# The first twelve steps' leaky ReLU: a maximum on VectorE, or a sum on GpSimd

## The chip, the core and the metric

The kernel runs on one core of a Trainium2 chip. The core has five engines that run side by side, each with its own queue of instructions that it takes strictly in order: TensorE (PE in the profile, its weight loads PEld), VectorE (DVE), ScalarE (ACT), GpSimd (POOL) and SyncE (SP), which here only issues DMAs. The metric is the device time of one execution in microseconds (us), as the median of several runs.

## The reference

Attention over 8 batches, 8 heads, 576 tokens and head size 64 feeds a feed-forward layer with 4608 tokens, model width 512 and 2048 hidden units:

```python
out_up    = repeat(softmax_attention(mean4(q), mean4(k), mean4(v)), 4)   # on 144 averaged tokens
out_local = attention over the keys at distance < 4
x = (out_up + out_local) as [4608, 512]
h = x @ w_in                                        # [4608, 2048]
g = maximum(h, 0) + alpha * minimum(h, 0)           # leaky ReLU, one slope alpha per hidden unit
out = g @ w_out                                     # [4608, 512]
```

All of it is in 32-bit floats. The kernel keeps that precision by splitting each operand of a large product into a high and a low part (names ending in h and l) and adding three products.

## The kernel before, in words

The tokens of the feed-forward layer are cut into 18 chunks of 256 (`T`), the hidden units into 16 blocks of 128. A *step* `st` does two hidden blocks of one chunk; there are 144 steps, eight to a chunk. Each step goes through five functions:

- `hidden(st)` (L743): 24 matmuls on TensorE make h of 128 x 512 in a PSUM tile `ph` (two buffers).
- `slopes(st)` (L756): ScalarE reads h twice for each block. `t` gets slope times h (L760), and h itself is overwritten with sign times h (L761). The columns `sign` (+1 or -1) and `slope` (alpha times sign) are made at the start, in `load_alpha`; the sign of a hidden unit with alpha above 1 is also multiplied into `w_out`.
- `larger(st)` (L763): VectorE takes the maximum of the two, which is the leaky ReLU up to that sign.
- `split(st)` (L766): ScalarE copies the result to `gh`, GpSimd subtracts to get `gl` (the helper `sub`, L69).
- `product(st)` (L786): 12 matmuls on TensorE add the step's share to the output tiles `o`. After eight steps `finish` copies these out through the tiles `sg` (L804).

Around the steps runs the attention. The first batch is done ahead of step 0. While the first steps run, three other things are in progress. The weights' last blocks are taken apart into high and low parts by `make` (L161): ScalarE starts each block (`temp<-raw`, L184), VectorE does four passes (L188 to L194) and a subtraction (L207 or L211), and ScalarE makes the high part in between (`wih`, `woh`, L199 and L203). The averaged attention of the next batches goes through `down` (L224) in pieces: GpSimd folds loaded rows together (`ld`, `s2q`, `s2k`, `s2v`, the helper `add`, L72), TensorE transposes (`qkT`, L250), ScalarE copies (`qd`, `kd`), TensorE makes the scores (`s`, L263), VectorE the maximum (`dnb`, L267), ScalarE exponentials and a scaling (`dp`, L273 and L282), TensorE transposes (`pT`, L287), ScalarE copies (`th`, L291), TensorE multiplies (`pv`, L297). These pieces share two PSUM banks (`bank("d", ...)`), so that a transpose waits for the copy that empties the bank. And the local attention of unit 3 (`local`, L566) begins on VectorE near step 9.

The order on each engine is written by hand: each function is put in a list with a time in steps (`at(s - 1.45, slopes, s)`, `at(s - 1.15, larger, s)`, `at(s - 1.0, split, s)`, L861 to L866), the list is sorted by that time, and the instructions are issued in that order. Only the part ahead of it, with the first batch and the first five pairs of weight blocks, is ordered by a scheduler, which may also set its last instructions among those of step 0 and step 1.

The tile `xf` (L665) of 128 x 512 in the pool `late` has one buffer and is written for the first time in unit 3, near step 13. The pool `late` takes over the memory of the pool `start`, in which the first batch lived.

Of the kernel before, what the change touches and what calls it, by code (L numbers as in the profile page):

```python
# [9 lines left out]
F32 = mybir.dt.float32  # L10
F32R = mybir.dt.float32r
I32 = mybir.dt.int32
AF = mybir.ActivationFunctionType
ALU = mybir.AluOpType
# [11 lines left out]
NF = DF // 128  # L26
# [16 lines left out]
T0_DEC, D_DEC = 0.5, 0.56  # L43
UNITS = {3: 7.5, 4: 12.2, 5: 17.4, 6: 22.7, 7: 28.0}
U_STEP = 5.92
BY_HALF = (5, 9, 13, 17, 21)
FAR = {3: 2, 4: 2, 5: 2, 6: 2}

# [2 lines left out]
def tile_attention_moe(ctx: ExitStack, tc: tile.TileContext, q, k, v, w_in, w_out, alpha, out):  # L51
    nc = tc.nc

    const = ctx.enter_context(tc.tile_pool(name="const", bufs=1))
# [16 lines left out]
    def add(o, a, b):  # L71
        nc.gpsimd.tensor_tensor(o, a, b, op=ALU.add)  # L72
# [33 lines left out]

    sign = const.tile([128, NF], F32, name="sign")
    slope = const.tile([128, NF], F32, name="slope")

    def load_alpha():  # L110
        nc.sync.dma_start(slope, alpha.rearrange("(f p) -> p f", p=128))
        nc.vector.tensor_scalar(sign, slope, 1.0, 2.0, op0=ALU.is_le, op1=ALU.mult)
        nc.vector.tensor_scalar(sign, sign, -1.0, None, op0=ALU.add)
        nc.vector.tensor_tensor(slope, slope, sign, op=ALU.mult)


    wi, wo = ([[None] * 4, [None] * 4] for _ in range(2))
# [448 lines left out]
    def local(u, t0, t1):  # L566
        b, jj = u // 3, u % 3
        st = {}
        near = 7 - FAR.get(u, 1)
        by_half = u in BY_HALF  # L570
        groups = ((0, 3), (3, 3)) if by_half else ((0, 4), (4, 2))
# [169 lines left out]
    gs, outs, hs = {}, {}, {}  # L741
# [13 lines left out]

    def slopes(st):  # L756
        t = gs[st] = two.tile([128, 2, T], F32, tag="t", name=f"t{st}")
        for j in range(2):
            f = 2 * (st % NP) + j
            nc.scalar.activation(t[:, j], hs[st][:, j], AF.Copy, scale=slope[:, f:f + 1])  # L760
            nc.scalar.activation(hs[st][:, j], hs[st][:, j], AF.Copy, scale=sign[:, f:f + 1])  # L761

    def larger(st):  # L763
        nc.vector.tensor_tensor(gs[st], hs.pop(st), gs[st], op=ALU.max)  # L764

    def split(st):  # L766
        t = gs[st]
# [59 lines left out]


    load_alpha()
    rest = two.tile([128, DM], F32, tag="stage", name="rest", bufs=SB)[:, 0:4 * (S - 2 * T)]  # L830
    rest = rest.rearrange("p (a n) -> p a n", a=4)
    nc.gpsimd.memset(qd32, 0.0)
    with tc.tile_pool(name="start", bufs=1) as start:
# [20 lines left out]
        def at(t, f, *args):  # L854
            events.append((t, len(events), f, args))
# [3 lines left out]
    late = ctx.enter_context(tc.tile_pool(name="late", bufs=1))  # L859

    for s in range(NS):  # L861
        at(s - 1.95, hidden, s)
        at(s - 1.45, slopes, s)
        at(s - 1.15, larger, s)
        at(s - 1.0, split, s)
        at(s + 0.6, product, s)  # L866
        if s % NP == NP - 1:
            at(s + 1.02, finish if s + 1 < NS else finish_last, s // NP)
# [20 lines left out]
    for u in range(len(UNITS) + 3, 3 * B + 1):  # L889
        begin[u] = begin[u - 1] + U_STEP  # L890
    for b in range(2, B):
# [8 lines left out]
    for u in range(3, 3 * B + 1):  # L900
        if u < 3 * B:
            when, *mine = local(u, begin[u], begin[u + 1])
        else:
            when = {"before 0": begin[u] + 0.8, "before 1": begin[u] + 1.2}
        if put and u - 1 in BY_HALF:
            at(begin[u] + 0.3, flip, 1)
# [36 lines left out]
```

## Time and profile before

| what | value |
|---|---|
| median of 3 runs | 1014.16 us (1013.35 to 1014.5) |
| the profiled execution's own time | 1012.62 us |
| its span | 1010.8 us, 17864 instructions |
| PE busy | 960.6 us (95%) |
| DVE busy | 832.8 us (82%) |
| ACT busy | 560.2 us (55%) |
| POOL busy | 482.1 us (48%) |

A share over the whole span is an average over stages. Step 0's matmuls begin at about 85 us, the twelfth step's slopes (step 11) at 168 us. What the change touches lies between these two. From there to the end TensorE has few gaps.

### The profile page before, as it was taken

The numbers are of one execution on the slowest core, as the hardware profiler recorded it, in microseconds if no ns is written. First come the engines' busy times: TensorE is split into PE (matmuls) and PEld (weight loads), VectorE is DVE, ScalarE is ACT, GpSimd is POOL, SyncE is SP. The second block draws the span as 40 slices with busy tenths as digits, with TensorE's granted clock in tenths as the row PEclk, the third lists the DMA queues.
The fourth block names the chain that finished last, engine by engine and source line by source line (L and its number), as shares of the span: only waits on it lengthen the run. The fifth ranks groups of instructions, "written<-read, shape, count | busy, mean of one in ns | idle before, by whom it ended". The sixth has DMA issues, their size and how long they took to land.

```text
span 1010.8 us, 17864 instructions
## 1 busy us (share of the span) xinstructions
PE 960.6 (95%) x6402; PEld 852.7 (84%) x6402; DVE 832.8 (82%) x1347; ACT 560.2 (55%) x1483; POOL 482.1 (48%) x612
## 2 busy tenths in 40 slices
PE   5877989999999999999999999999999999999998
PEld 4756878898888898988888888888988898989997
DVE  6899988899888899899888898898898899997111
ACT  4767766465565555555455555555555554444442
POOL 2040645677665546555554544656555543323221
PEclk9856989999999999999999999999999999999999
DMA  8946443232422322433322332322331412210000
GB/s 191 222 148 242 123 153 98 83 119 83 145 83 73 118 81 78 121 97 93 103 88 66 100 111 71 125 80 74 123 100 60 131 49 61 86 43 22 1 21 22
DMA packets 61218, 98.26 MB, mean 97 GB/s; under 512 B 21578, under 2 KB 26954, under 8 KB 61130
## 3 DMA queue, kind: packets, MB, share of 16 engines
q1 hardware_dynamic: 60938, 96.87, 32.0%
q8 instruction: 50, 0.82, 0.3%
q10 hardware_dynamic: 192, 0.26, 0.1%
q14 instruction: 38, 0.31, 0.1%
HBM read 87.67 MB, written 9.44 MB: 96 GB/s over the span
## 4 chain that ended last, share of the span: by engine, by line
PE 72%; DVE 15%; ACT 4%; issue 3%; DMA 2%; POOL 2%; SPq 2%; DVEq 0%; ACTq 0%; POOLq 0%
PE o L798 33%; PE h L752 33%; DMA raw<-in_moe_w_out 2%; DVE qk L591 2%; DVE lb L650 2%; PE s L263 2%; DVE t L764 1%; PE pv L297 1%; DVE ls L595 1%; DVE temp L193 1%; DVE pv L647 1%; PE xp L659 1%; PE pT L287 1%; DVE temp L194 1%; DMA ld<-in_q 1%
## 5 line engine op out<-in xcount | busy, mean ns | idle before, releaser
L69 POOL TENSOR_TENSOR gl<-t,gh 128x512 fp32r<-128x512 f32 x144 | 186.5, 1295 | 390.8 <-ACT gh L769 347.4
L760 ACT ACTIVATE t<-h,slope 128x256 f32<-128x256 f32 x288 | 136.3, 473 | 203.0 <-PE h L752 166.2
L764 DVE TENSOR_TENSOR t<-h,t 128x512 f32<-128x512 f32 x144 | 99.0, 687 | 113.2 <-ACT h L761 108.6
L752 PE MATMUL h<-xh,wih 128*128 128x256 f32 x1152 | 190.9, 287 | 0.7 <-ACT xh L518 0.7
L798 PE MATMUL o<-woh,gh 128*128 128x512 f32 x576 | 188.1, 407 | 0.4 <-ACT woh L203 0.4
L752 PE MATMUL h<-xl,wih 128*128 128x256 f32 x1152 | 183.7, 281 | 0.6 <-POOL xl L69 0.6
L752 PE MATMUL h<-xh,wil 128*128 128x256 f32 x1152 | 184.1, 282 | 0.0
L798 PE MATMUL o<-wol,gh 128*128 128x512 f32 x576 | 182.1, 397 | 0.1
L798 PE MATMUL o<-woh,gl 128*128 128x512 f32 x576 | 182.1, 397 | 0.0
L752 PEld LDWEIGHTS h<-xh,wih 128*128 128x128 f32 x1152 | 163.5, 190 | 10.5 <-issue 1.8
L72 POOL TENSOR_TENSOR ld<-ld 72x256 f32<-72x256 f32 x168 | 125.4, 747 | 73.9 <-DMA ld<-in_q 49.4
L752 PEld LDWEIGHTS h<-xl,wih 128*128 128x128 f32 x1152 | 156.9, 190 | 0.8 <-POOL xl L69 0.8
L752 PEld LDWEIGHTS h<-xh,wil 128*128 128x128 f32 x1152 | 157.3, 190 | 0.0
L769 ACT CAST gh<-t 128x512 fp32r<-128x512 f32 x144 | 89.1, 619 | 118.7 <-DVE t L764 68.4
L595 DVE TENSOR_REDUCE ls<-qk 128x12 f32<-128x768 f32 (+1 forms) x126 | 136.4, 1083 | 2.8
L798 PEld LDWEIGHTS o<-woh,gl 128*128 128x128 f32 x576 | 108.6, 189 | 26.4
L798 PEld LDWEIGHTS o<-wol,gh 128*128 128x128 f32 x576 | 108.4, 188 | 26.4 <-DVE wol L211 0.7
L761 ACT ACTIVATE h<-h,sign 128x256 f32<-128x256 f32 x288 | 126.4, 439 | 0.0
L650 DVE TENSOR_TENSOR lb<-lb,pv 128x384 f32<-128x384 f32 x202 | 113.9, 564 | 5.5
L798 PEld LDWEIGHTS o<-woh,gh 128*128 128x128 f32 x576 | 98.3, 189 | 16.3 <-issue 2.2
L647 DVE TENSOR_TENSOR pv<-v,lb 128x1152 f32<-128x1152 f32 x84 | 93.6, 1115 | 2.6
L591 DVE TENSOR_TENSOR qk<-k,qp 128x768 f32<-128x768 f32 (+1 forms) x78 | 84.0, 1077 | 0.0
(148 smaller groups left out, 1111.4 us busy)
## 6 DMA issues: line engine op xcount, KB each, us to landing
k<-in_k SPq DMA_DIRECT2D x41, 384.0 KB
v<-in_v SPq DMA_DIRECT2D x41, 384.0 KB
raw<-in_moe_w_in SPq DMA_DIRECT2D x16, 512.0 KB
raw<-in_moe_w_out SPq DMA_DIRECT2D x16, 512.0 KB
ld<-in_q SPq DMA_DIRECT2D x56, 144.0 KB
ld<-in_k SPq DMA_DIRECT2D x56, 144.0 KB
ld<-in_v SPq DMA_DIRECT2D x56, 144.0 KB
q<-in_q SPq DMA_DIRECT2D x42, 192.0 KB
```

The costliest lines, as they stand in the source:

```text
L69: nc.gpsimd.tensor_tensor(o, a, b, op=ALU.subtract)
L72: nc.gpsimd.tensor_tensor(o, a, b, op=ALU.add)
L591: nc.vector.tensor_tensor(st["pr"][:, :nd], window(tiles[u, "k"], half, d0, nd), st["qp", half].unsqueeze(1).to_broadcast([128, nd, 2, 192 ...
L595: nc.vector.tensor_reduce(out=st["s"][:, half, d0:d0 + nd, :].rearrange("p a b -> p (a b)"), in_=st["pr"][:, :nd].rearrange("p a h (t d) - ...
L647: nc.vector.tensor_tensor(st["pr"][:, :nd], window4(tiles[u, "v"], half, d0, nd), prob(half, d0, nd), op=ALU.mult)
L650: nc.vector.tensor_tensor(st["acc"], st["acc"], st["pr"][:, i], op=ALU.add)
L752: nc.tensor.matmul(ph[:, j], w[:, m, 128 * o:128 * o + 128], x[:, m, :], start=(i == 0), stop=(i == 11))
L760: nc.scalar.activation(t[:, j], hs[st][:, j], AF.Copy, scale=slope[:, f:f + 1])
L761: nc.scalar.activation(hs[st][:, j], hs[st][:, j], AF.Copy, scale=sign[:, f:f + 1])
L764: nc.vector.tensor_tensor(gs[st], hs.pop(st), gs[st], op=ALU.max)
L769: nc.scalar.copy(gh, t)
L798: nc.tensor.matmul(outs[c][m], g[:, j, 128 * m:128 * m + 128], wo[w][n][:, o, :], start=(f == 0 and i == 0), stop=(f == NF - 1 and i == 2))
```

## The change

For the first twelve steps (`EARLY = 12`) the leaky ReLU is formed as a sum: with `gain` = sign - slope, which is never negative, max(sign h, slope h) is slope h + relu(gain h). ScalarE writes slope times h to `t` as before, and relu(gain h) to a tile `sh` in SBUF, which is the one buffer of the tag `xf`. GpSimd adds the two. The other 132 steps are unchanged.

```diff
+EARLY = 12
...
+        nc.vector.tensor_tensor(gain, sign, slope, op=ALU.subtract)
...
     def slopes(st):
         t = gs[st] = two.tile([128, 2, T], F32, tag="t", name=f"t{st}")
+        other = hs[st]
+        if st < EARLY:
+            other = late.tile([128, 512], F32, tag="xf", name=f"sh{st}").rearrange("p (j n) -> p j n", j=2)
         for j in range(2):
             f = 2 * (st % NP) + j
             nc.scalar.activation(t[:, j], hs[st][:, j], AF.Copy, scale=slope[:, f:f + 1])
-            nc.scalar.activation(hs[st][:, j], hs[st][:, j], AF.Copy, scale=sign[:, f:f + 1])
+            if st < EARLY:
+                nc.scalar.activation(other[:, j], hs[st][:, j], AF.Relu, scale=gain[:, f:f + 1])
+            else:
+                nc.scalar.activation(other[:, j], hs[st][:, j], AF.Copy, scale=sign[:, f:f + 1])
+        if st < EARLY:
+            hs[st] = other

     def larger(st):
-        nc.vector.tensor_tensor(gs[st], hs.pop(st), gs[st], op=ALU.max)
+        if st < EARLY:
+            add(gs[st], hs.pop(st), gs[st])
+        else:
+            nc.vector.tensor_tensor(gs[st], hs.pop(st), gs[st], op=ALU.max)
```

The order of the matmuls and of SyncE's DMAs is the same as before. On the other engines it moves at these places (numbers in names are buffers; a slope, `t`, `sh` and `gl` of the same step stand near each other).

ScalarE at steps 0 and 1, before: `t<-h,slope` and `h<-h,sign` of the two halves of step 0, then a weight block (`temp`), and so on to step 1 and to the exponentials (`dp,dsm`) of a piece of the averaged attention.

```order
L760 ACTIVATE t_995<-h_970,slope 128x256
L761 ACTIVATE h_970<-h_970,sign 128x256
L760 ACTIVATE t_995<-h_970,slope 128x256
L761 ACTIVATE h_970<-h_970,sign 128x256
L184 ACTIVATE temp<-raw_4_881 128x1024
...
L761 ACTIVATE h_1011<-h_1011,sign 128x256
L273 ACTIVATE dp_0_1060,dsm_0_1055<-s_0_1042,dnb_0_1054 96x144 x3
L275 ACTIVATE dsm_0_1055<-dsm_0_1055 96x3
L203 ACTIVATE woh_889<-temp,sign 128x512 x2
L769 CAST gh_1065<-t_1048 128x512
```

The same place now:

```order
L766 ACTIVATE t_997<-h_972,slope 128x256
L187 ACTIVATE temp<-raw_4_883 128x1024
L768 ACTIVATE sh_998<-h_972,gain 128x256
L766 ACTIVATE t_997<-h_972,slope 128x256
L768 ACTIVATE sh_998<-h_972,gain 128x256
...
L768 ACTIVATE sh_1052<-h_1014,gain 128x256
L206 ACTIVATE woh_891<-temp,sign 128x512 x2
L276 ACTIVATE dp_0_1064,dsm_0_1059<-s_0_1045,dnb_0_1058 96x144 x3
L278 ACTIVATE dsm_0_1059<-dsm_0_1059 96x3
L783 CAST gh_1069<-t_1051 128x512
```

The weight block has moved ahead of three of step 0's four activations, and the high part of a weight (`woh`) ahead of the exponentials.

GpSimd from step 0 to step 2, before: the two `gl` of steps 0 and 1, four folds, the `gl` of step 2.

```order
L69 TENSOR_TENSOR gl_1008<-t_995,gh_1007 128x512
L69 TENSOR_TENSOR gl_1066<-t_1048,gh_1065 128x512
L72 TENSOR_TENSOR ld_1_0_1040<-ld_1_0_1040 72x2x128
L72 TENSOR_TENSOR s2q_1_1094<-ld_1_0_1040 72x2x64
L72 TENSOR_TENSOR ld_1_1_1046<-ld_1_1_1046 72x2x128
L72 TENSOR_TENSOR s2q_1_1094<-ld_1_1_1046 72x2x64
L69 TENSOR_TENSOR gl_1144<-t_1107,gh_1143 128x512
```

The same place now:

```order
L73 TENSOR_TENSOR t_997<-sh_998,t_997 128x512
L70 TENSOR_TENSOR gl_1011<-t_997,gh_1010 128x512
L73 TENSOR_TENSOR t_1051<-sh_1052,t_1051 128x512
L70 TENSOR_TENSOR gl_1070<-t_1051,gh_1069 128x512
L73 TENSOR_TENSOR ld_1_0_1043<-ld_1_0_1043 72x2x128
L73 TENSOR_TENSOR s2q_1_1098<-ld_1_0_1043 72x2x64
L73 TENSOR_TENSOR ld_1_1_1049<-ld_1_1_1049 72x2x128
L73 TENSOR_TENSOR s2q_1_1098<-ld_1_1_1049 72x2x64
L73 TENSOR_TENSOR t_1111<-sh_1112,t_1111 128x512
L70 TENSOR_TENSOR gl_1149<-t_1111,gh_1148 128x512
```

Each step's sum stands ahead of its `gl`, and behind the folds that were issued before it.

GpSimd at steps 8 to 10, before: the last folds of a piece (`s2v`), the low part of the first batch's remaining tokens (`xl<-rest,xh`), the `gl` of steps 9 and 10.

```order
L72 TENSOR_TENSOR ld_3_5_1634<-ld_3_5_1634 72x2x128
L72 TENSOR_TENSOR s2v_3_1698<-ld_3_5_1634 72x2x64
L69 TENSOR_TENSOR xl_1735<-rest,xh_1734 128x4x64
L69 TENSOR_TENSOR gl_1750<-t_1712,gh_1749 128x512
L69 TENSOR_TENSOR gl_1836<-t_1799,gh_1835 128x512
```

The same place now:

```order
L73 TENSOR_TENSOR ld_3_5_1645<-ld_3_5_1645 72x2x128
L73 TENSOR_TENSOR s2v_3_1709<-ld_3_5_1645 72x2x64
L70 TENSOR_TENSOR xl_1747<-rest,xh_1746 128x4x64
L73 TENSOR_TENSOR t_1723<-sh_1724,t_1723 128x512
L70 TENSOR_TENSOR gl_1762<-t_1723,gh_1761 128x512
L73 TENSOR_TENSOR t_1811<-sh_1812,t_1811 128x512
```

The sum of step 9 stands behind `xl<-rest,xh`, and the `gh` that ScalarE makes from it is read by the `gl` behind it.

## Rows read from the trace of the kernel before

**Rows 1.** The page, 40 slices of the span: granted TensorE clock in tenths.

```profile
PEclk9856989999999999999999999999999999999999
```

**Rows 2.** Stretches in us: busy time of PE, PEld, DVE, ACT, POOL; clock; DMA.

```profile
85.00:165.00 80.00, 71.56 (x443) 62.00 (x445) 69.85 (x103) 56.54 (x142) 34.99 (x48) 0.92 0.48 152
...
300.00:1010.00 710.00, 699.45 (x4657) 625.49 (x4655) 569.74 (x912) 373.60 (x993) 336.82 (x410) 1.00 0.25 78
```

**Rows 3.** Waits of PE, 84 to 200 us: total, times, longest.

```profile
PE s L263 <- ACT kd L258: 3.4, 2, 2.1
...
PE qkT L250 <- ACT th L291: 1.7, 1, 1.7
PE pT L287 <- ACT dp L282: 1.5, 1, 1.5
PE qkT L250 <- POOL gl L69: 1.0, 1, 1.0
...
PE o L798 <- ACT woh L203: 0.4, 1, 0.4
```

**Rows 4.** The page's costliest groups: count, busy us, mean ns, idle before.

```profile
L69 POOL TENSOR_TENSOR gl<-t,gh 128x512 fp32r<-128x512 f32 x144 | 186.5, 1295 | 390.8 <-ACT gh L769 347.4
L760 ACT ACTIVATE t<-h,slope 128x256 f32<-128x256 f32 x288 | 136.3, 473 | 203.0 <-PE h L752 166.2
L764 DVE TENSOR_TENSOR t<-h,t 128x512 f32<-128x512 f32 x144 | 99.0, 687 | 113.2 <-ACT h L761 108.6
...
L761 ACT ACTIVATE h<-h,sign 128x256 f32<-128x256 f32 x288 | 126.4, 439 | 0.0
```

**Rows 5.** Timeline, steps 0 and 1: start us, duration us, engine, line, operation.

```profile
90.96 1.19 ACT L184 ACTIVATE temp<-raw 128x1024 f32<-128x1024 f32 x1
...
93.35 1.22 DVE L207 TENSOR_TENSOR wil<-temp,wih 128x1024 fp32r<-128x1024 f32 x1
...
93.91 1.78 POOL L69 TENSOR_TENSOR gl<-t,gh 128x512 fp32r<-128x512 f32 x1 [31.63 <-ACT gh L769]
...
94.49 1.76 DVE L189 TENSOR_SCALAR temp<-temp 128x1024 int32<-128x1024 int32 x1
...
98.53 1.21 DVE L194 SCALAR_TENSOR_TENSOR temp<-raw,temp 128x1024 int32<-128x1024 int32 x1
...
102.28 1.01 ACT L282 ACTIVATE dp<-dp,drs 96x144 f32<-96x144 f32 x3
```

**Rows 6.** Timeline, steps 2 to 4.

```profile
105.94 0.62 ACT L769 CAST gh<-t 128x512 fp32r<-128x512 f32 x1 [0.57 <-DVE t L764]
106.11 0.46 POOL L72 TENSOR_TENSOR s2q<-ld 72x128 f32<-72x128 f32 x1
...
114.49 0.70 DVE L188 TENSOR_SCALAR temp<-temp 128x512 f32<-128x512 f32 x1 [1.30 <-ACT temp L184]
```

**Rows 7.** Timeline, step 8.

```profile
149.96 0.68 DVE L764 TENSOR_TENSOR t<-h,t 128x512 f32<-128x512 f32 x1
```

**Rows 8.** Timeline, step 9.

```profile
158.79 0.42 ACT L824 CAST xh<-rest 128x256 fp32r<-128x256 f32 x1
...
159.29 0.75 POOL L69 TENSOR_TENSOR xl<-rest,xh 128x256 fp32r<-128x256 f32 x1 [1.03 <-ACT xh L824]
159.36 0.62 ACT L769 CAST gh<-t 128x512 fp32r<-128x512 f32 x1
159.89 1.06 ACT L804 COPY sg<-o 128x512 f32<-128x512 f32 x2
...
160.84 0.70 ACT L291 COPY th<-pT 72x288 f32<-72x288 f32 x2
...
161.38 0.32 PE L250 MATMUL qkT<-ident,s2q 72*128 72x72 f32 x2 [0.99 <-POOL gl L69]
```

**Rows 9.** Timeline, matmul pairs of `product` at two clocks.

```profile
114.39 0.63 PE L798 MATMUL o<-woh,gh 128*128 128x512 f32 x2
...
136.75 1.05 PE L798 MATMUL o<-woh,gh 128*128 128x512 f32 x2
```

More of the change, by code (lines that the diff above doesn't have):

```diff
@@ L108, in tile_attention_moe @@
     slope = const.tile([128, NF], F32, name="slope")
+    gain = const.tile([128, NF], F32, name="gain")
     def load_alpha():
```

## The prediction

> **What bounds the kernel now.** I first read the stretches [rows 2]. From 300 us on TensorE is busy 699 of 710 us, so the end moves by whatever TensorE gains or loses before that: a matmul stream that starts a microsecond later ends about a microsecond later. From 85 to 165 us, which holds steps 0 to 10, TensorE is busy 71.6 of 80 us at a granted clock of 0.92, and VectorE 69.9 of 80. So the stretch is VectorE's, but not all of it is TensorE's loss. The second view is TensorE's own waits there [rows 3]. None of them names the maximum `t` (L764). They name ScalarE's copies for the averaged attention: `kd` (two, 2.1 us at 92 us and 1.3 at 123), `dp` (1.5 at 134), `th` (1.7 at 141), one put down to `gl` (1.0 at 161), and `woh` 0.4. The five after 100 us come to 5.9 us. All hang on ScalarE's queue, and ScalarE waits in turn for VectorE's weight passes and, at each `gh`, for the maximum. The third view is the clock [rows 1]: it falls in slices 2 to 4 and again in slice 6. A pair of `product` matmuls takes 1.05 us instead of 0.63 at the lower level (1.2 GHz instead of 2.4) [rows 9]; a step's `product` has six pairs, of which four or so fall into one such stretch, so a stretch costs about 4 x 0.42 = 1.7 us.
>
> **What the change removes and adds.** VectorE loses twelve maxima of 0.687 us, 8.2 us in all; GpSimd gains twelve sums. No row shows this sum; the nearest is the subtraction `gl` of the same size, 1.295 us [rows 4], and one such instruction at 1.78 us [rows 5] is the other end. I take 1.29, so 15.5 us on an engine that is busy 35 of 80 us [rows 2]: it fits, and where it stands in the queue decides. ScalarE's Relu into SBUF should lie between the 0.439 us of `h<-h,sign` and the 0.473 of `t<-h,slope` [rows 4]. I take 0.473: 24 x 0.034 = 0.8 us spread over twelve steps. At the other end it gains nothing and loses nothing. The built program has one table load on ScalarE in both versions. `gain` is one VectorE instruction long before step 0: nothing. The PSUM tile of h comes free without the maximum, but as no TensorE wait names `t`, that is worth nothing.
>
> A `gh` now waits for a GpSimd sum instead of a VectorE maximum, and behind `gh` in ScalarE's queue stand weight blocks, `qd`, `kd`, `th` and the next slopes. TensorE's `product` comes about 1.6 steps after `gh`, so the later `gl` itself costs nothing; what counts is ScalarE's queue.
>
> **Steps 0 and 1: +2.6 us.** `sh` and the rest of step 0's slopes now stand behind `temp` (1.19 us from 90.96), so the sum can begin at about 93.3. From there VectorE has three 1.2 us passes with both operands in SBUF. The rows show what a GpSimd pass does beside such work [rows 5]: `gl` became ready at 93.9 while `wil` ran to 94.57, and took 1.78 us instead of 1.29; the pass L189 behind it took 1.76 us, more than the 1.22 of the pass with two operands ahead of it. `gl` ended 1.1 us after `wil`, and L189 0.6 us after `gl`: each waited for the other. So they exclude each other. Before, L194 ended at 98.53 + 1.21 = 99.74. Two maxima fall out of VectorE's queue (-1.3), two sums get in its way (+2 x 1.25): 100.9. `woh` (two casts, 1.3 us) now goes ahead of the exponentials, which begin at 102.25 and take 1.25; then 0.2 for `dsm`, 0.6 for `gh`, 0.6 for `temp`: `dp` at 104.9 instead of 102.28. TensorE waits for it: +2.6.
>
> The Trainium skill (page "SBUF — State Buffer", section "SBUF: two separate sides") has the rule behind this: GpSimd and a VectorE instruction in a two-port mode or with two SBUF inputs hold one shared port pair as an exclusive lock for a whole instruction. Rows 5 agree. By that rule the weight passes from step 2 on do not collide, since their `temp` lies in PSUM. Were there no lock, this term would be about +0.1 instead of +2.6 and the total would fall to about +1.6.
>
> **Steps 2 to 7: most of it is absorbed, +0.9 left.** At step 2 the sum stands behind `gl` of step 1 and four folds, so `gh` comes at about 109.3 instead of 105.94 [rows 6]: +3.4 on ScalarE. VectorE's wait of 1.30 us at 114.49, ScalarE's own wait for the maximum before the `gh` of step 3, and the maxima that are gone (0.6 us each at VectorE's pitch) take this back: I get +1.7 at step 4's slopes, +1.2 at `kd` (123 us), +0.9 at `dp` (134) and at `th` (141). TensorE's own +2.6 meets waits of 1.3, 1.5 and 1.7 us at these three places [rows 3], so it follows ScalarE: +0.9 at 141. VectorE's relief goes into waits for `temp`, `wih` and `woh`, which ScalarE makes later; that is why 8.2 us less work does not become 8.2 us.
>
> **Step 8: -0.6 us.** The maximum at 149.96 [rows 7] stands between two weight passes on the way to `dnb`, the exponentials, `woh`, `dp` and the slopes of step 9. `slopes` of step 8 waits for TensorE, and GpSimd has time for its sum, so here the maximum really leaves the path: +0.3 left.
>
> **Step 9: +2.0 us.** Before, `gh` began at 159.36, when the maximum was done and `xh` (158.79 + 0.42 = 159.21) was too [rows 8]. Now the sum stands behind `xl<-rest`, which needs that `xh`: 159.29 + 0.75 = 160.04, then 1.29 for the sum, so `gh` at 161.35: +2.0. Behind it are `sg` (1.06) and `th` (0.70). The `qkT` at 161.38 needs the bank that `th`'s first copy empties (160.84 + 0.35, about 161.2); `gl`, which the row names, ended at the same moment, but it is no operand. TensorE has already waited 0.99 us there, so nothing absorbs this: it restarts at 163.7.
>
> From 163 to 191 us TensorE has no wait, VectorE's unit 3 waits for TensorE's `s` and slopes, and moves with it. **Sum: 2.6 - 1.7 - 0.6 + 2.0 = +2.3 us** on the profiled execution's 1012.62 (span 1010.8 and 1.8 around it): 1014.9. The median of the runs lies 1.54 us above that execution, so I forecast 1014.16 + 2.3 = 1016.5. About 2 us (0.2%) is what a measurement here can tell from no change.
>
> **Rivals.** *Faster.* VectorE holds the weight passes in this stretch, and if ScalarE's waits for it shrink by more than the sums add (GpSimd done early, because it is half idle), TensorE's 5.9 us of waits go down by half and one low-clock stretch goes with them: -3.0 - 1.7 = -4.7, 1009.5. For it: VectorE is the busiest engine but one, and several maxima stand right between weight passes. Against: the order puts sums behind folds and behind `xl`, and no TensorE wait names `t`.
>
> *Slower by more.* TensorE's wait at 161 us grows from 1.0 to about 2.9 us. The waits of 2.1, 1.5 and 1.7 us at 92, 134 and 141 us were each followed by a stretch at the lower clock [rows 1, 3]; those of 1.3 and 1.0 us were not. If the long wait at 161 brings one more, that is +1.7; if the sum of step 6 also stays behind the fold that waits for its load near 133 us and pushes `dp` and `th` by 1.5, the total is 2.3 + 1.7 + 1.5 = +5.5, 1019.7. It decides from a wait of about 1.5 us on. Against: a wait of 1.7 us at 192 us was followed by full clock.
>
> *A wash.* `xl` and the sum find their operands earlier than I think, or the gain of step 8 repeats at steps 5 and 7: -2.0 against +2.3, 1014.5.
>
> **Chances.** The forecast 0.45, with its own range from 1014.7 to 1018.7; faster 0.2; slower by more 0.2; a wash 0.15. Of the forecast's own range some 60% lies beyond +2 us. So slower by over 0.2%: 0.27 + 0.2 = 0.47; within 0.2%: 0.18 + 0.15 = 0.33, and a little of the faster case, 0.34; faster 0.19. The range reaches from the faster case to above the slower one: 1009.5 to 1021.
>
> **What will show it.** Right: the two sums of steps 0 and 1 beside VectorE passes of over 2 us; `dp` of the first piece near 105 us; TensorE's `qkT` of the fourth piece at 163 to 164 us with a wait of 2 to 3 us, and ScalarE's `gh` of step 9 there waiting for GpSimd; VectorE's busy time down by 8 us and more waits on ScalarE. Wrong: if that `qkT` runs by 161 us, the term of step 9 is wrong; if the waits at 123 to 141 us are shorter than before, VectorE's relief reached TensorE; if TensorE is at the lower clock after 164 us, the slower case holds.

## The result and the profile after

The changed kernel takes 1017.26 us (median of six runs, 1015.98 to 1020.58) against 1014.32 us for the kernel before on the same chip. The ratio is 1.0031, with an interval from 1.0016 to 1.0046: it is slower by about 3 us. The forecast was 1016.5 us, that is +2.3 us.

The profiled execution of the changed kernel took 1020.58 us (span 1018.5), 7.96 us more than that of before. That is more than the runs differ by, so the first question is how much of it belongs to the change. I compare where TensorE is at fixed places of the program: the first matmul `h` of step 0, and the first matmul of `product` in steps 3, 7, 8, 12, 64, 72 and 141. The table gives the time between two such places in the kernel before, and then how much longer it is in each other profile (us; read from TensorE's rows in the timelines). It has all the kernels of this text; the ones not named yet are explained below.

| profile | step 0 begins | to step 3 | 3 to 7 | 7 to 8 | 8 to 12 | 64 to 72 | steps 0 to 12 together |
|---|---|---|---|---|---|---|---|
| before (its times) | 85.23 | 33.66 | 34.22 | 8.52 | 26.10 | 53.16 | 102.50 |
| before, once more | -0.23 | +0.04 | -0.02 | -0.01 | +0.01 | -0.05 | +0.02 |
| after | +3.77 | +3.16 | -3.29 | +1.03 | +1.50 | +1.50 | +2.40 |
| after, once more | -1.65 | +2.12 | -2.23 | +1.02 | +1.49 | +1.58 | +2.40 |
| sums in 0, 1 | -1.67 | +1.64 | +1.26 | -0.01 | -0.01 | +0.06 | +2.88 |
| sums in 2 to 11 | -1.68 | +0.31 | -1.54 | +1.24 | +1.33 | +0.03 | +1.34 |
| sum in 9 alone | +0.49 | +0.27 | +1.12 | +2.02 | +1.28 | +0.04 | +4.69 |
| all but 9 | -1.06 | +1.61 | -0.39 | -0.78 | -0.02 | +1.61 | +0.42 |
| sums in 2 to 8 | -2.41 | +2.06 | -3.21 | -0.79 | -0.01 | +1.59 | -1.95 |
| the same, `xl` early | -2.17 | +0.35 | +0.56 | -0.78 | -0.01 | +1.59 | +0.12 |
| all, `xl` late | -1.16 | +1.61 | -1.78 | +1.53 | +1.32 | +0.03 | +2.68 |
| all, `xl` early | +1.67 | +3.13 | -2.56 | +0.12 | +1.50 | +1.58 | +2.19 |
| sum on VectorE | -2.20 | +0.07 | -0.16 | -0.22 | -0.01 | +0.03 | -0.32 |
| no sum at all | -1.02 | -0.43 | -3.42 | -1.10 | -0.02 | +1.60 | -4.97 |

Three things are to be seen. The late start of the first profile of after (+3.77) is not the change's: its second profile starts 1.65 us before the kernel before. The stretch of the change costs +2.40 us in both profiles of after. And some columns hold pieces of 1.3 to 1.6 us that come and go: stretches at the lower clock. Outside these columns, from step 12 to 64 and from 72 to 141, before and after agree within 0.1 us (all but 9 alone loses 2.05 us between steps 12 and 64, where it has one more such stretch, near 263 us).

The page of after, to be set beside [rows 1], shows the clock below 9 in slices 3 and 4 alone. The stretch behind step 9 lies in slice 7 and is too short to show there, so the windows and the timeline have to be read:

```profile
PEclk9957999999999999999999999999999999999999
```

The stretches, as in [rows 2] (busy time of PE, PEld, DVE, ACT, POOL; clock; DMA). Since step 0 began 3.77 us later, the first and the last row hold another piece of the program than those of before; the row between them is the first one moved by that much. In it TensorE's clock is 0.91 instead of 0.92, VectorE's busy time is 1.6 us less and GpSimd's 13.5 us more than in [rows 2].

```profile
85.00:165.00 80.00, 67.85 (x425) 59.98 (x425) 68.24 (x96) 54.39 (x134) 46.49 (x57) 0.89 0.48 151
88.77:168.77 80.00, 70.08 (x432) 61.91 (x433) 68.21 (x95) 55.50 (x141) 48.51 (x58) 0.91 0.48 149
300.00:1010.00 710.00, 702.73 (x4680) 629.37 (x4679) 574.08 (x919) 378.88 (x1008) 339.11 (x414) 1.00 0.25 79
```

TensorE's waits of after, 84 to 200 us, beside [rows 3] (total, times, longest). The wait put down to `gl` has gone from 1.0 to 2.8 us, that for `th` from 1.7 to 2.6; `woh` is gone. The wait for `dp` is another one than before: it lies at 108 us, for the first piece. The waits of 1.3 us for `kd` at 123 us and of 1.5 us for `dp` at 134 us are gone.

```profile
...
PE qkT L253 <- POOL gl L70: 2.8, 1, 2.8
PE qkT L253 <- ACT th L294: 2.6, 1, 2.6
PE s L266 <- ACT kd L261: 2.3, 1, 2.3
...
PE pT L290 <- ACT dp L285: 1.6, 1, 1.6
```

The sums of after, from the view of one tile (shortest, median and longest duration in ns; first and last start), beside the `gl` and the maximum of [rows 4]. The price taken, 1.29 us, is the median.

```profile
L70 POOL TENSOR_TENSOR gl<-t,gh x144: 1266/1292/1480, 99.2 to 1009.3; 128x512 fp32r<-128x512 f32 x144
L73 POOL TENSOR_TENSOR t<-sh,t x12: 1268/1286/1552, 96.9 to 176.2; 128x512 f32<-128x512 f32 x12
```

The timeline of after at steps 0 and 1 (start, duration, engine, line, operation), beside [rows 5]. Three VectorE passes that take 1.22 us alone take 2.18 to 2.30 us. Each began beside a GpSimd instruction and ended 1.08 to 1.09 us after it: 98.47 and 99.56, 100.69 and 101.77, 102.91 and 103.99.

```profile
96.92 1.55 POOL L73 TENSOR_TENSOR t<-sh,t 128x512 f32<-128x512 f32 x1 [29.82 <-ACT sh L768]
97.38 2.18 DVE L196 SCALAR_TENSOR_TENSOR temp<-raw,temp 128x1024 int32<-128x1024 int32 x1
...
99.21 1.48 POOL L70 TENSOR_TENSOR gl<-t,gh 128x512 fp32r<-128x512 f32 x1 [0.73 <-ACT gh L783]
99.48 2.29 DVE L210 TENSOR_TENSOR wil<-temp,wih 128x1024 fp32r<-128x1024 f32 x1
...
101.45 1.46 POOL L73 TENSOR_TENSOR t<-sh,t 128x512 f32<-128x512 f32 x1 [0.77 <-ACT sh L768]
101.69 2.30 DVE L197 SCALAR_TENSOR_TENSOR temp<-raw,temp 128x1024 int32<-128x1024 int32 x1
...
107.65 1.01 ACT L285 ACTIVATE dp<-dp,drs 96x144 f32<-96x144 f32 x3
...
110.95 1.27 POOL L73 TENSOR_TENSOR t<-sh,t 128x512 f32<-128x512 f32 x1
111.40 0.70 DVE L192 TENSOR_SCALAR temp<-temp 128x512 int32<-128x512 int32 x1
112.26 0.62 ACT L783 CAST gh<-t 128x512 fp32r<-128x512 f32 x1 [1.63 <-POOL t L73]
```

The last three rows are step 2 [rows 6]: the sum takes 1.27 us and the weight pass beside it 0.70 us, so here neither waits for the other. The subtraction `wil`, which took 2.29 us above, takes 0.69 us on its half-size block beside the next `gl`:

```profile
112.96 1.29 POOL L70 TENSOR_TENSOR gl<-t,gh 128x512 fp32r<-128x512 f32 x1 [0.73 <-ACT gh L783]
...
113.39 0.69 DVE L210 TENSOR_TENSOR wil<-temp,wih 128x512 fp32r<-128x512 f32 x1 [1.30 <-ACT wih L202]
```

With the start's 3.77 us taken off, `dp` is at 103.88 us, 1.6 later than before, and `gh` of step 2 at 108.49, 2.55 later.

Step 9 of after, beside [rows 8] and [rows 9]: the sum stands behind `xl`, `gh` waits 2.09 us for it, `sg` and `th` follow, TensorE waits 2.83 us, and then the pairs of `product` take 1.05 us.

```profile
161.53 0.41 ACT L838 CAST xh<-rest 128x256 fp32r<-128x256 f32 x1
...
162.02 0.74 POOL L70 TENSOR_TENSOR xl<-rest,xh 128x256 fp32r<-128x256 f32 x1 [0.92 <-ACT xh L838]
...
162.72 1.27 POOL L73 TENSOR_TENSOR t<-sh,t 128x512 f32<-128x512 f32 x1
...
164.03 0.62 ACT L783 CAST gh<-t 128x512 fp32r<-128x512 f32 x1 [2.09 <-POOL t L73]
...
165.51 0.70 ACT L294 COPY th<-pT 72x288 f32<-72x288 f32 x2
166.05 0.32 PE L253 MATMUL qkT<-ident,s2q 72*128 72x72 f32 x2 [2.83 <-POOL gl L70]
...
166.94 1.05 PE L812 MATMUL o<-wol,gh 128*128 128x512 f32 x2
167.80 1.05 PE L812 MATMUL o<-woh,gl 128*128 128x512 f32 x2
168.65 1.05 PE L812 MATMUL o<-woh,gh 128*128 128x512 f32 x2
```

### The profile page after: what moved, and what is told of

Its sections match the earlier page's. It is cut to its first block, busy times and chain, and to the rows that moved or that the text cites. A ratio compares the mean times of both kernels' runs of the same rounds, so it can differ in the third digit from the quotient of the medians.

```text
span 1018.5 us, 17849 instructions
## 1 busy us (share of the span) xinstructions
PE 966.1 (95%) x6402; PEld 858.8 (84%) x6402; DVE 828.8 (81%) x1336; ACT 560.5 (55%) x1483; POOL 502.6 (49%) x624
## 4 chain that ended last, share of the span: by engine, by line
PE 75%; DVE 13%; ACT 4%; issue 2%; SPq 2%; DMA 1%; POOL 1%; DVEq 0%; ACTq 0%; POOLq 0%
PE h L755 34%; PE o L812 33%; DVE lb L653 2%; DVE qk L594 2%; PE s L266 2%; PE pv L300 2%; DVE ls L598 1%; PE pT L290 1%; DVE pv L650 1%; DVE t L778 1%; PE xp L662 1%; ACT t L766 1%; DVE temp L196 1%; SPq L396 1%; PE fs L448 1%
## 5 line engine op out<-in xcount | busy, mean ns | idle before, releaser
L778 DVE TENSOR_TENSOR t<-h,t 128x512 f32<-128x512 f32 x132 | 90.9, 688 | 114.3 <-ACT h L770 109.1
L73 POOL TENSOR_TENSOR ld<-ld 72x256 f32<-72x256 f32 x168 | 129.1, 769 | 72.9 <-DMA ld<-in_q 48.4
L770 ACT ACTIVATE h<-h,sign 128x256 f32<-128x256 f32 x264 | 116.0, 439 | 0.0
```

The lines of the kernel that those rows point to most:

```text
L770: nc.scalar.activation(other[:, j], hs[st][:, j], AF.Copy, scale=sign[:, f:f + 1])
```

## The experiments

My theory was the forecast's: the sums lose at steps 0 and 1 and at step 9, and gain a little in between. The rivals were that VectorE's relief decides, that the new order on ScalarE decides, or that all of it is the clock. In most kernels the only edit is the set of steps that use the sum, with `st < EARLY` turned into `st in EARLY`.

**Step 9 by itself.** Two kernels, one with the maximum at step 9 alone, one with the sum there alone:

```diff
-EARLY = 12
+EARLY = (0, 1, 2, 3, 4, 5, 6, 7, 8, 10, 11)     # all but 9
+EARLY = (9,)                                    # 9 alone
```

> The sums of steps 0 to 8, 10 and 11 stay on GpSimd; step 9 has its maximum on VectorE again. Theory 1 (step 9's sum waits behind the low part of the remaining tokens and holds ScalarE, then TensorE, by 1.9 us, and a stretch at the lower clock follows the long wait): gh of step 9 no longer waits for GpSimd, TensorE's wait at the fourth qkT falls from 2.8 to about 1 us or less, no low clock after it, and the time is 0 to 1 us below the kernel before (ratio 0.999 to 1.000). Rival (the sums cost a little in every step, by the shared access of GpSimd and VectorE and by ScalarE's queue): 11 of 12 parts of the loss stay, ratio 1.002 to 1.003.

> Only step 9 is a sum on GpSimd; the eleven others have their maximum on VectorE. Theory 1: the loss is all here, and without the 0.9 us that the steps before gained: the fourth qkT is 1.9 us later than in the kernel before and TensorE waits 2.9 us for it; +1.9 us, or +3.4 with a stretch at the lower clock after it: ratio 1.002 to 1.0035. Rival (a little in every step): 1.0002.

Measured: all but 9 takes 1014.47 us, ratio 0.9989 (0.9969 to 1.0009); 9 alone takes 1017.44 us, 1.0027 (1.0008 to 1.0046). In the table the columns from step 7 to step 12 separate them without overlap. With the sum at step 8 and the maximum at 9, steps 7 to 8 take 0.78 us less than before, and the clock stays full. With the sum at 9 alone they take 2.02 us more, and steps 8 to 12 another 1.28. So the sum of step 9 costs 3.3 us by itself: 1.8 of waiting (2.82 us against 0.99) and 1.5 of low clock, which begins before step 8's `product`. TensorE's row at step 9, first of 9 alone, then of all but 9:

```profile
165.07 0.47 PE L253 MATMUL qkT<-ident,s2q 72*128 72x72 f32 x2 [2.82 <-POOL gl L70]
```

```profile
160.76 0.32 PE L253 MATMUL qkT<-ident,s2q 72*128 72x72 f32 x2 [1.00 <-POOL gl L70]
```

**What the sum of step 9 stands behind.** All twelve sums, but the `xl` of the remaining tokens issued behind the sum and `gl` of step 9; then the same with the whole of `place_rest` issued 0.57 of a step earlier, at 7.25 instead of 7.82.

```diff
         nc.scalar.copy(hi, rest)
+
+    def rest_low():                        # late
+        hi, lo = (t[:, :, 0:S - 2 * T] for t in operand(2))
         sub(lo, rest, f32(hi))
...
+    at(8.02, rest_low)
```

```diff
-    at(decoded + 0.6, place_rest)
+    at(7.25, place_rest)                   # early
```

> All twelve sums as in the change, but the low part of the remaining tokens (xl<-rest,xh) is issued behind the sum and gl of step 9 instead of ahead of them. Theory 1: the sum of step 9 runs as soon as sh is written, gh of step 9 begins about 0.7 us after that of a maximum would, at most 0.5 us of TensorE's time is lost there, no low clock, and the time is within 1 us of the kernel before (ratio 0.999 to 1.0005). Rival (a little in every step, or GpSimd too busy): still 1.002 to 1.003.

> The changed kernel with all twelve sums, but the remaining tokens' copy (xh<-rest) and subtraction (xl) are issued at step 7.25, between a weight's high part and the scaling of dp, so that GpSimd has xl behind it long before the sum of step 9. Theory 1 (step 9 loses because its sum stands behind xl, and because the second sg needs the buffer that rest holds until xl has run): gh of step 9 starts within 0.3 us of xh's old place, qkT of the fourth piece waits about 1.0 us instead of 2.8, no low-clock stretch follows; the 1.0 + 1.5 us of step 9 come back: 1014.5 to 1015 if nothing else changes, ratio about 1.000 to 1.0005. Theory 2 (step 9 loses because a GpSimd sum of 1.27 us stands where a maximum of 0.69 stood, whatever is ahead of it): the wait stays at 2 us or more, 1016.5 to 1017.5, ratio 1.002 to 1.003.

Measured: late 1016.58 us, 1.0014 (0.9994 to 1.0034); early 1015.02 us, 0.9997 (0.9975 to 1.0018). Late, `gh` waits 0.69 us for its sum and no more, yet TensorE still waits 3.11 us. The reason stands on ScalarE, in the timeline of that kernel: the second copy into `sg` waits for `xl`.

```profile
157.66 0.62 ACT L783 CAST gh<-t 128x512 fp32r<-128x512 f32 x1 [0.69 <-POOL t L73]
158.19 0.58 ACT L818 COPY sg<-o 128x512 f32<-128x512 f32 x1
...
159.59 0.73 POOL L70 TENSOR_TENSOR xl<-rest,xh 128x256 fp32r<-128x256 f32 x1
160.35 0.58 ACT L818 COPY sg<-o 128x512 f32<-128x512 f32 x1 [1.58 <-POOL xl L70]
160.83 0.69 ACT L294 COPY th<-pT 72x288 f32<-72x288 f32 x2
161.38 0.47 PE L253 MATMUL qkT<-ident,s2q 72*128 72x72 f32 x2 [3.11 <-ACT th L294]
```

`rest` lies in one of the two buffers of `stage` that `sg` takes, so `xl` has to run before `th` either way: behind the sum it delays `th`, ahead of it `gh`. Early, it is out of the way of both, and steps 7 to 8 take 0.91 us less than in after. But neither theory's number came: the wait is 1.92 us. The timeline of the early kernel shows what is left.

```profile
159.38 0.46 ACT L768 ACTIVATE sh<-h,gain 128x256 f32<-128x256 f32 x1
...
159.98 0.46 POOL L73 TENSOR_TENSOR s2v<-ld 72x128 f32<-72x128 f32 x1
...
160.40 1.30 POOL L73 TENSOR_TENSOR t<-sh,t 128x512 f32<-128x512 f32 x1
...
161.72 0.62 ACT L783 CAST gh<-t 128x512 fp32r<-128x512 f32 x1 [1.50 <-POOL t L73]
...
163.75 0.32 PE L253 MATMUL qkT<-ident,s2q 72*128 72x72 f32 x2 [1.92 <-POOL gl L70]
```

The sum's second operand is there at 159.84; the folds and the `s2v`, which now run behind `xl`, keep GpSimd until 160.4, and the sum takes 1.30 us where a maximum takes 0.69. From the first slope of step 9 to its `gh` it is 2.51 us before, 4.33 in after, 3.41 here. So 0.9 of the 1.8 us was `xl`, and the rest is the folds and the sum's own length. The low clock came all the same (+1.50).

**The engine or the operation.** The sum on VectorE in the maximum's place, ScalarE's work as in after; and a kernel that leaves out both the maximum and the sum in the first twelve steps, so that `gh` is made from the slope part alone.

```diff
-            add(gs[st], hs.pop(st), gs[st])
+            nc.vector.tensor_tensor(gs[st], hs.pop(st), gs[st], op=ALU.add)     # on VectorE
+            hs.pop(st)                                                          # none at all
```

> The changed kernel with its Relu parts, but the sum of the two parts on VectorE in the place of the maximum; GpSimd does what it did before. Theory 1 (GpSimd costs it: the exclusive port at steps 0 and 1 and the place behind xl at step 9): without GpSimd's sums the starts of product agree with the kernel before within 0.5 us after step 9, the wait of qkT is about 1.0 us, ratio 0.999 to 1.0005 (1013.5 to 1015). Theory 2 (ScalarE's new order and form, temp ahead of step 0's slopes, Relu into SBUF, cost it): it stays slower than before, 1016 to 1017.5, ratio 1.0015 to 1.003. The sum of 128x512 with both operands in SBUF should take 0.65 to 0.70 us on VectorE, or over 1.2 where it meets a GpSimd pass.

> Neither maximum nor sum in the first twelve steps: gh is made from slope times h alone, so the join of the leaky ReLU is left out there. This is what VectorE's relief is worth when nothing takes its place. Theory 1: TensorE regains its waits between 123 and 161 us in part, 1 to 3 us below the kernel before (ratio 0.997 to 0.999). Rival (VectorE's maxima bound the stretch): 5 us or more below (0.995 or less). If the relief is worth nothing at all: 1.000.

Measured: on VectorE 1011.99 us, 0.9971 (0.9947 to 0.9994); none at all 1008.21 us, 0.9938 (0.9916 to 0.9960). On VectorE the sum takes 0.68 us, ScalarE's order is that of after, and TensorE is within about 0.3 us of the kernel before at each place of the table, so ScalarE's new order and the Relu cost nothing, and what after loses is lost on GpSimd. The measured time of that kernel lies lower than its trace explains; its step 0 began 2.2 us early, which I can tie to no edit, and I leave the rest open. With none at all, steps 0 to 12 are 5.0 us shorter. That is what the relief would be worth in this stretch if nothing had to take the maximum's place and `gh` waited for no join. It is more than I had allowed for, and the GpSimd sums take all of it back and more.

**Steps 0 to 8.** Sums in steps 0 and 1 alone, in 2 to 11, and in 2 to 8:

```diff
-EARLY = 12
+EARLY = (0, 1)
+EARLY = (2, 3, 4, 5, 6, 7, 8, 9, 10, 11)
+EARLY = (2, 3, 4, 5, 6, 7, 8)
```

> Sums in steps 0 and 1 only. Theory 1 (a sum beside two-operand passes of VectorE costs TensorE 1.5 to 3 us by step 3, and a part of it is absorbed by the waits at 123 to 141 us): first matmul of step 0 to product of step 3 takes 1.5 to 3.2 us more than in the kernel before, of which 1 to 1.5 us are left at step 7; step 9 as before; 1015 to 1017, ratio 1.0005 to 1.0025. Theory 2 (it is absorbed in full, as the changed kernel's trace by itself would say): step 7 within 0.3 us of before, 1014 to 1015.

> Sums in steps 2 to 11 only; steps 0 and 1 keep the maximum. Theory 1 (the loss of steps 0 and 1 is absorbed by step 7, the loss of step 9 is not): product of step 1 starts about 3 us earlier than in the changed kernel relative to step 0, but by step 7 at most 0.5 us of it is left, the wait at step 9 is 2.5 us or more with low clock behind it: 1016 to 1017.5, ratio 1.002 to 1.003. Theory 2 (the loss of steps 0 and 1 reaches the end, as TensorE's waits are only refilled by it): 1013.5 to 1015, ratio 0.9995 to 1.0005.

> Sums in steps 2 to 8 only; steps 0, 1, 9, 10 and 11 keep the maximum. Theory 1 (sums help where GpSimd has room and cost at 0, 1 and 9): steps 2 to 8 give TensorE back 1 to 2 us by VectorE's relief, step 9 as before: 1012.5 to 1014, ratio 0.998 to 0.9995, the best of the versions with sums. Theory 2 (VectorE's relief never reaches TensorE, whatever the step): 1014 to 1015, ratio 0.9995 to 1.0005.

Measured: 0 and 1 alone 1014.82 us, 1.0008 (0.9987 to 1.0029); 2 to 11 1016.98 us, 1.0013 (0.9992 to 1.0033); 2 to 8 1014.09 us, 0.9982 (0.9962 to 1.0003). In the first the timeline shows the same pair as in after, and TensorE's wait for `dp`:

```profile
96.01 1.47 POOL L73 TENSOR_TENSOR t<-sh,t 128x512 f32<-128x512 f32 x1 [0.77 <-ACT sh L768]
96.25 2.31 DVE L197 SCALAR_TENSOR_TENSOR temp<-raw,temp 128x1024 int32<-128x1024 int32 x1
...
102.22 1.01 ACT L285 ACTIVATE dp<-dp,drs 96x144 f32<-96x144 f32 x3
...
102.67 1.14 PE L290 MATMUL pT<-ident,dp 96*72 96x96 f32 x6 [1.54 <-ACT dp L285]
```

Its step 0 began 1.67 us before that of the kernel before, so `dp` is 1.6 us late, as in after. That holds in all six profiles with sums in steps 0 and 1: `dp` begins 18.64 to 18.66 us after step 0's first matmul, against 17.05 and 17.07 in the two of before. Step 3 is 1.64 us late, step 7 2.90. Sums in 2 to 11 are 1.23 us ahead at step 7 and then lose 2.57 to step 12. But how much of the first is left at step 7 a single trace can't tell: the two kernels with sums in 2 to 8 have nearly the same work up to there, and stand at -1.15 and +0.91; the one with the sum at 9 alone works like before up to step 8, and stands at +1.39. The difference is where low-clock stretches fall, and whether a wait that would have come anyway hides them. The expected gain of 1 to 2 us for 2 to 8 is within its interval, and so is nothing.

**A version to beat both.** Sums in 2 to 8 and `place_rest` early:

```diff
-EARLY = 12
+EARLY = (2, 3, 4, 5, 6, 7, 8)
...
-    at(decoded + 0.6, place_rest)
+    at(7.25, place_rest)
```

> Sums in steps 2 to 8 only, maxima in the others, and the remaining tokens' copy and subtraction issued at step 7.25. Theory 1 (step 9's gh waits for the copy xh before it, so without it gh, sg, th and qkT all come about 0.4 us earlier): step 7 to step 12 takes 1.0 to 1.4 us less than before, the wait of qkT is 0.4 to 0.8 us, no low clock behind it: 1011.5 to 1013.5, ratio 0.9970 to 0.9990. Theory 2 (VectorE's relief is all there is): as with sums in steps 2 to 8 alone, 1013 to 1014.5, ratio 0.9985 to 1.0.

Measured: 1012.84 us, 0.9974 (0.9957 to 0.9992), the lowest ratio of the kernels that keep sums on GpSimd, but its interval overlaps that of sums in 2 to 8 alone. The time is as theory 1 had it, the mechanism is not: TensorE's wait at step 9 is 1.00 us as before. Without `xh` ahead of it, `gh` waits for the maximum itself, which begins 0.10 us after its second operand and takes 0.69 us; `gh` begins 2.51 us after the first slope of step 9, as before. What its trace does show as a gain is the 0.78 us of step 8; over steps 0 to 12 together it is at +0.12, so why the median is lower stays open.

**The same kernels once more**, one profiled execution each.

> The changed kernel once more, one profiled execution, for what belongs to the execution and what to the program. If the late start of the first profile of the changed kernel (step 0 begins 3.8 us later than in the profile of before) belongs to the execution, step 0 begins elsewhere between 82 and 89 us, while step 7 to step 12 takes 2.3 to 3.3 us more than before, with low clock behind the wait at step 9. If it belongs to the change, step 0 begins at 88 to 90 us again.

> The kernel before once more, one profiled execution. The wait at step 9 should be 1.0 us again with full clock behind it; the start of step 0 may lie anywhere from 82 to 89 us, and a low-clock stretch of 1.5 us may or may not follow the 2.5 us wait at 530 us. A stretch of steps 0 to 7 that differs from the first profile by over 1 us would be one low-clock stretch more or less.

Measured: 1015.26 us (span 1013.2) and 1012.48 us (span 1010.6). Step 0 begins at 83.58 and 85.00 us, while steps 0 to 12 take +2.40 and +0.02 us. So 3.77 of the 7.96 us between the first two profiles were the execution's, 2.40 the change's, and 1.50 a low clock at 530 us, of which more below; of the last 0.29, 0.26 lie outside the span.

## Why the prediction was right

The sum said +2.3 us; the trace says +2.40 in this stretch, twice. The terms of steps 8 and 9 were right, and the mechanism of steps 0 and 1. Two errors of opposite sign cancelled, so that the sum came out within 0.1 us is luck.

- **Steps 0 and 1, +2.6.** The mechanism was right: the sums and the two-operand passes exclude each other. The Trainium skill (page "SBUF — State Buffer", section "SBUF: two separate sides") calls the shared port an exclusive lock for a whole instruction; the passes that end 1.1 us after a GpSimd instruction agree, and so do sums of 1.27 us beside passes of 0.70 from step 2 on, whose `temp` is in PSUM. The size was off: `dp` is 1.6 us late and not 2.6, 0.7 of which is that L197 ended 0.5 us later than before (103.99 - 3.77 against 99.74) and not 1.2. In three of the six kernels with these sums TensorE is 1.6 us late at step 3, too; what made it 2.1 to 3.2 us in after is a longer low clock.
- **Steps 2 to 7, -1.7.** Measured -3.3 and -2.2, so nothing was left at step 7 (-0.13 and -0.11) where I had +0.9. The prediction had this sign of being wrong, and it came: the waits at 123, 134 and 141 us, 4.5 us together, shrank to 2.6 us in after and 3.5 in its second profile, so VectorE's relief did reach TensorE. A low-clock stretch went as well: between steps 3 and 7 TensorE's clock is 0.90 before and 0.94 in after. It is 0.90 in all five profiles whose maximum or sum runs on VectorE in these steps, and 0.94 or 0.95 in seven of the nine that don't (0.90 in all but 9 and in sums in 2 to 8 with `xl` early). The sum of the forecast had put this at nothing; it is the mechanism of the rival *faster*. With no sum at all step 7 is 3.9 us early: what I had as lost in waits for ScalarE reaches TensorE when no sum stands in its way. Here are steps 3 to 7 of before and of after, columns as in [rows 2]:

```profile
118.89:153.11 34.22, 29.66 (x177) 25.36 (x175) 29.24 (x47) 22.38 (x57) 16.61 (x24) 0.90 0.47 143
```

```profile
125.82:156.75 30.93, 28.04 (x177) 24.48 (x175) 24.26 (x38) 21.89 (x60) 19.69 (x26) 0.94 0.47 141
```

- **Step 8, -0.6.** Measured -0.78 or -0.79 in the three kernels with the maximum at step 9.
- **Step 9, +2.0.** In after, 1.03 + 0.78 = 1.81 (the gain of step 8 taken out); alone, a wait that is 1.83 us longer. The chain through `xl`, `gh`, `sg` and `th` was as written. I had not seen that `sg` needs the buffer of `rest`. The `qkT` that was to run at 163 to 164 us ran at 162.28, the late start taken off, as nothing of the loss was left at step 7.
- **The step that failed** is "from 163 to 191 us TensorE has no wait", read as full clock. The low clock of the rival *slower by more* came: +1.50 where that had 1.7. All six profiles with the sum at step 9 have it, after waits of 1.92 to 3.11 us; none of the eight others has it, with waits of 1.00 us or less. The rival's other part, the sum of step 6 behind a fold, did not show as a loss: step 7 stands even. Its bound, a wait of about 1.5 us, is not one: see the last section.

So the error of about -1.0 us up to step 7 (+0.9 forecast, -0.13 measured) and that of +1.5 us behind step 9 cancel but for the smaller ones. VectorE's busy time fell by 4.0 us and not by the 8 that were to show the forecast right, because the three stretched passes of steps 0 and 1 put 3.4 us on top (the groups `temp<-raw,temp` and `wil<-temp,wih` rose by 2.3 and 1.1 us, the maxima fell by 8.1); the rest are small groups of both signs. That the measured median rose by 2.9 us and not by 2.4 lies within the interval; whether the low clock at 530 us has a part in it is open.

## What to carry to other kernels

Work moved to a half-idle engine pays where that engine's queue is empty at that moment, step by step: ask of each moved instruction what stands ahead of it there, and what stands behind its reader on the next engine. An instruction that is ahead in the way may not simply go behind, if a buffer that it frees is needed soon. A TensorE wait that grows can cost its length again in clock, so price both.

## What the runs showed of the hardware

- A wait's length does not settle whether the lower clock follows. Behind the `h` of step 1 TensorE waits 2.13 us for `kd` in before and then runs at the lower level (groups of four `h` matmuls take 1.05 us); at the same place of after it waits 2.35 us, and they take 0.63 us. Before, then after:

```profile
94.65 1.34 PE L263 MATMUL s<-kd,qd 128*96 128x144 f32 x6 [2.13 <-ACT kd L258]
...
96.65 1.05 PE L752 MATMUL h<-xh,wil 128*128 128x256 f32 x4
```

```profile
99.95 0.98 PE L266 MATMUL s<-kd,qd 128*96 128x144 f32 x6 [2.35 <-ACT kd L261]
...
101.24 0.63 PE L755 MATMUL h<-xh,wil 128*128 128x256 f32 x4
```

- Nor is the same wait always followed by it. At about 530 us TensorE waits 2.4 to 2.5 us for `lb` in every profile; in seven of fourteen it then ran at a clock of 0.93 over the 25 us (1.00 in the others), and steps 64 to 72 took 1.5 to 1.6 us more. Both profiles of after have it and neither of before, but among the others kernels with sums are on both sides, and so are those with no sum on GpSimd; what decides stays open. Here are the windows of after and of before from 520 to 545 us:

```profile
520.00:545.00 25.00, 22.50 (x146) 20.08 (x145) 19.25 (x35) 13.19 (x35) 14.80 (x19) 0.93 0.33 104
```

```profile
520.00:545.00 25.00, 22.51 (x160) 20.05 (x159) 20.73 (x36) 13.25 (x36) 12.62 (x16) 1.00 0.28 85
```

- The part ahead of step 0, to which the change adds one small VectorE instruction (`gain`), ended between 82.8 and 89.0 us in the fourteen profiles, and differently for one program (89.00 and 83.58). Two single profiles are therefore compared by stretches, not by their ends.
